# Routing attention and a PReLU feed-forward layer on one core: another order for seeded products, for the pairs' ordering, and for the weight conversions

## The chip, the cores and the metric

The kernel runs on one core of one Trainium2 chip. The metric is device time in microseconds (us) of one execution; the lower, the better. The engines are named as the profile names them: PE (TensorE matmuls), PEld (its weight loads), DVE (VectorE), ACT (ScalarE), POOL (GpSimd) and SP (SyncE, here a queue that issues DMAs). PE writes only to PSUM, which is dealt out in banks of 512 floats on 128 partitions. Each engine works through its own instructions in the order in which the program emits them; an instruction that waits holds all that stand behind it on the same engine.

## The reference

Attention in which a query sees only the keys of its own cluster, and then a feed-forward layer with a PReLU:

```python
B, H, S, D = 4, 8, 768, 64           # 16 clusters per head
q_assign = np.argmax(np.einsum('bhsd,hcd->bhsc', q_n, c_n), axis=-1)
k_assign = np.argmax(np.einsum('bhsd,hcd->bhsc', k_n, c_n), axis=-1)
mask = q_assign[:, :, :, None] == k_assign[:, :, None, :]
scores = np.where(mask, scale * np.matmul(q, k.transpose(0, 1, 3, 2)), -1e9)
attn = softmax(scores)
x = np.matmul(attn, v).transpose(0, 2, 1, 3).reshape(B * S, H * D)   # 3072 x 512
h = x @ w_in                                                          # 512 x 2048
out = (np.maximum(h, 0) + alpha * np.minimum(h, 0)) @ w_out           # 2048 x 512
```

q_n, k_n and c_n are q, k and the centroids, normalised. The weights and alpha come from the host in 64-bit floats (w_in, w_out as pairs of 32-bit words), and the kernel makes 32-bit floats of them on the chip.

## The kernel before

**Pairs and steps.** Work is cut into 16 pairs (a batch and two heads), four to a batch. The pairs n = 0 to 7 (batches 0 and 1, `NO = 8`) are done whole: each in two halves of the queries, each half in three steps. The pairs n = 8 to 15 (batches 2 and 3) are first brought into the order of their clusters; then a tile of queries only meets its neighbouring tiles of keys ("near"), and a pair takes three steps. So there are 72 steps, u = 0 to 71; pair n of the last eight starts at step 48 + 3(n - 8).

**Slots and ticks.** Everything is written out by hand in the order in which it is to be issued. `tick()` counts slots, runs what `later(slots, piece)` has put off, and issues up to two waiting loads. Steps 0 to 23 (the first part, batch 0) have five ticks each: scores (`score`, L815, masks L824, exponentials L833 and L836), then `weigh` of the step before (denominators L946, products with v L953), then three slots. When a half has ended, DVE turns its denominators (L959), inverts and spreads them (L965, L969, L926) and normalises (L1050); the next half's L946 needs the one denominator bank, and its L953 needs a bank back.

From step 24 on (`TOGETHER`) three steps make a group: the first begins with a head (three ticks: two thirds of the scores with the weighing of the pair before, its normalising, then the last third of the scores), followed by slots 3 and 4; the other two have slots 0 to 4. In every slot, after the due pieces, come one piece of the pair's own work, up to two pieces of `sorting`, in every third slot a weight conversion, and then pieces of the feed-forward layer of an earlier batch, as many as bring the rest down to the slot's share (`feed_down_to`). In a head step `prepare` runs before these pieces, in the other steps after them.

**Feed-forward.** The first product is done by Strassen's scheme in Winograd's form: for each pair of column blocks, seven products p1 to p7 of 768 columns (L1111) on three PSUM banks a, z, e. p1 fills a and ACT copies it to z (L1125); p6 adds onto a, p2 onto z, p5 fills e; p7 and p3 add onto a and e. DVE adds the results (L1096), ACT copies them out (L1130, L1134, L1139, L1157), and DVE applies the slope (L1100). p4 of a column pair, which adds onto a once DVE has read it, is kept pending and done within the next column pair, after three of its products (`settle`). The weights' sums come from DRAM, two forms to a load (`fetch_sums`, on ACT's queue), four such tiles in turn; a tile is fetched when an older one has been used up. The second product is L1183, in parts of four matmuls of 512 columns; `ps_f` has five banks for all of this, `ps_m` one (`misc`).

**Conversions.** `convert` loads raw words through SP's queue (L253) and makes floats in three pieces: split (DVE, L259 and L261), scale (ACT, L265 and L267), join (DVE, L271, L274, L277). In the first part one begins in each step: 16 blocks of w_in, whose sums `quarters` forms (L318) and stores, and then 8 blocks of w_out, 512 wide. In steps 24 to 47 follow 16 halves of 256 columns, one in every third slot, with two raw tiles.

**Ordering.** For the last eight pairs: `order_features` (L626), `order_sims` (L635, in the misc bank), `order_counts` (argmax L453 to L461, by cluster L644, running counts L649, one piece a slot), `order_begins` (L661, misc bank), `order_ranks` (L669 to L671), `order_rows` (L678 to L682) and `order_clusters` (L701 to L707), then `order_stage` (SP) and `order_scatter` (POOL, L728) through `sorting`; `order_load` fetches the rows back three steps before the pair starts, and `prep_clusters` (L493, misc bank) spreads the clusters. `ORDERS` holds the step at which each pair's ordering begins. In a head, `weigh_near`'s second side (L986) uses the misc bank until `normalise_near` (L992) has read it. `to_rows` (L1015, copied by L1018) and `put_back` (POOL, L1023) return a near pair's rows to their places.

**The end.** After step 71 the rest of batch 2's layer is dealt out while the last pair is put back; then batch 3's layer starts, some 25 small DVE instructions check that the assumptions held (L1441 to L1487), and one matmul (L1491) gathers the flag. If it fails, a general version runs; with these inputs it doesn't.

Of the kernel before, what the change touches and what calls it, by code (L numbers as in the profile page):

```python
# [23 lines left out]
def kernel(  # L24
# [68 lines left out]
    def later(slots, piece):  # L93
        due.setdefault(now[0] + slots, []).append(piece)
# [110 lines left out]
    for i in range(10):  # L205
        nc.tensor.matmul(out=warm[:, 0:P], lhsT=ident, rhs=ident, start=True, stop=True)

    inverses = const.tile([P, 2 * NCH, HS // Q], FP32, name="inverses")
    cn = inverses.rearrange("p n x -> p (n x)")[:, 0:D]
    cs2 = const.tile([P, 1], FP32, name="cs2")  # L210
# [123 lines left out]
    W_IN = len(sources) * 4  # L334
    for x0 in range(0, NQ, FQ):
        for f in (*range(x0, x0 + FQ), *range(NQ + x0, NQ + x0 + FQ)):
            n = CW if x0 == 0 else CW // 2
            for n0 in range(0, CW, n):
                sources.append((w_out_words[f * P:(f + 1) * P, 2 * n0:2 * (n0 + n)],
                                w_out_sb[:, f, n0:n0 + n], None))  # L340
# [6 lines left out]
        return coming.popleft()  # L347
    fetched, under_way = deque(), deque()
    begun, converted, first_ends = [0], [0], [1 << 20]
    limit = [W_IN + 2 * FQ]  # L350

    def fetch(ahead):

# [191 lines left out]
    def second_part():  # L545

        first_part.close()
        for name, bufs in (("gpool", NQ), ("ypool", NJ), ("emore", 1), ("ordc", 1),
                           ("ordp", 1), ("order", NCH + 2)):
            sorts[name] = fast.enter_context(tc.tile_pool(name=name, bufs=bufs))  # L550
        for i in range(2):
            e_tiles.insert(0, sorts["emore"].tile([P, 2, HS], FP32, name=f"more{i}"))
        fast.enter_context(middle)
        cvt[0] = middle.enter_context(tc.tile_pool(name="cvt2", bufs=2))
        raw2 = middle.enter_context(tc.tile_pool(name="raws2", bufs=1))
        raw_tiles[:] = [raw2.tile([P, CW // 2, 2], U32, name=f"raw{5 + i}") for i in range(2)]
        limit[0], first_ends[0] = W_IN + 2 * FQ + 4 * FQ, now[0]

    def third_part():
        middle.close()  # L560
# [79 lines left out]
    def order_counts(n, ps):  # L640

        top, first, pieces = argmax(ps, exact=True)
        member = sorts["ordp"].tile([P, HS], BF16, name="mine")
        pieces.append(lambda: nc.vector.transpose(  # L644
            out=member, in_=top.rearrange("p t c -> p (t c)")))

        def scan():
            count = sorts["ordp"].tile([P, HS], FP32, name="count")
            nc.vector.tensor_tensor_scan(count, member, member, 0.0, ALU.add, ALU.max)  # L649
            us[n] = member, count  # L650
        pieces.append(scan)
        for i, piece in enumerate(pieces):

            later(i if i < len(pieces) - 2 else i + 2, piece) if i else piece()
        later(len(pieces) + 4, lambda: order_begins(n))

    def order_begins(n):
        member, count = us[n]
# [38 lines left out]
    def order_clusters(n, begin):  # L697
        ordp, order = sorts["ordp"], sorts["order"]

        begun = ordp.tile([P, HS], BF16, name="mine")  # L700
        nc.vector.tensor_scalar(out=begun, in0=sorts["place"], scalar1=begin[:, 0:1],  # L701
                                scalar2=None, op0=ALU.is_ge)
        begunT = asg.tile([P, 2 * NX, NC], BF16, name="top")
        nc.vector.transpose(out=begunT.rearrange("p t c -> p (t c)"), in_=begun)
        first = order.tile([P, 2 * NX], BF16, name="cluster")
        with nc.allow_low_precision(reason="integers up to 16"):
            nc.vector.tensor_reduce(out=first, in_=begunT, axis=AX.X, op=ALU.add)  # L707
        firsts[n] = first
# [82 lines left out]
    waiting, weighed = [], {}  # L791
    e_tiles = [epool.tile([P, 2, HS], FP32, name=f"E{i}") for i in range(2 * GROUP)]

    def score(n, half, chunks):


        qkT = qkTs[n]
# [13 lines left out]
        for c, ps in zip(chunks, pss):  # L811
            tokens, m = queries(c)
            for h in range(2):
                r = h * D
                nc.tensor.matmul(  # L815
                    out=bank(ps, h, m),
                    lhsT=qkT[r:r + D, S + c * P:S + (c + 1) * P],
                    rhs=qkT[r:r + D, tokens], start=True, stop=not early_mask)
        if early_mask:
            for h in range(2):  # L820
                for c, ps in zip(chunks, pss):
                    g, i = divmod(NJ + c, GT)
                    r = slice(g * Q, (g + 1) * Q)
                    nc.tensor.matmul(  # L824
                        out=bank(ps, h), lhsT=members[n][1][r, h, i * P:(i + 1) * P],
                        rhs=aqs[n, half][r, 0, :], start=False, stop=True)
# [162 lines left out]
    def normalise_near(n):  # L989
        outT = inp.tile([P, 2, NJ, D], FP32, name="qk").rearrange("p h j d -> p (h j d)")  # L990
        for side in range(2):
            nc.vector.tensor_tensor(out=outT[:, side * HS:(side + 1) * HS],  # L992
                                    in0=pos.pop((n, side))[:, 0:HS],
                                    in1=rds.pop((n, side)), op=ALU.mult)
        whole = tc.dram_tile([2 * S, D], FP32, name=f"back{n}")
        to = dram_disjoint_views(whole, 2 * NJ)
        found = orders.pop(n)
        place = sorts["order"].tile([P, 2, NJ], I32, name="place")
        nc.vector.tensor_scalar(out=place, in0=found[:, :, :, 0], scalar1=0, scalar2=S - 1,
                                op0=ALU.max, op1=ALU.min)  # L1000
        rows = sorts["byrow"].tile([P, NJ, P], FP32, name="rows")

        starts = (6, 9)
        for i in range(2):
            later(starts[i], lambda i=i: to_rows(outT, rows, i))
            for x in range(NJ):
                later(starts[i] + 2 + x // 2,
                      lambda i=i, x=x: put_back(to, place, rows, i * NJ + x))
        later(starts[1] + 2 + HJ, lambda: fetch_back(n, whole))
# [69 lines left out]
    def ffn_pieces(b):  # L1079
# [23 lines left out]
        def hidden(x):  # L1103
# [14 lines left out]
            def p1():  # L1118
# [4 lines left out]
                    gs[f] = sorts["gpool"].tile([P, 2, HS], FP32, name="gT")  # L1123
                product(a, A11, B11, True)
                nc.scalar.copy(bank(z), bank(a))  # L1125
                rest.extend([p6, p2, p5, settle] if pending else [p5, p6, p2])

            def p6():
                product(a, S2, T2, False)
# [108 lines left out]
    FREE = SLOTS * SB - 3  # L1238


    ORDERS = [24, 27, 30, 33, 39, 42, 45, 48]
    prep_at, load_at = {}, {}
    for (n, half), u in start_of.items():
        def at(step, slot, piece):
            prep_at.setdefault((step, slot), []).append(piece)
        if half is None:
            t = ORDERS[n - NO]
            load_at.setdefault(t, []).append(lambda n=n: load(n))
            for i in range(2):
                at(t + 2, 2 + 2 * i, lambda n=n, i=i: order_features(n, i))  # L1250
            at(t + 3, FIRST + 1, lambda n=n: order_sims(n))
            load_at.setdefault(u - 3, []).append(lambda n=n: order_load(n))
            at(u - 4, 0, lambda n=n: prep_clusters(n))
            for i in range(2):
                at(u - 1, i, lambda n=n, i=i: order_blocks(n, i))
                at(u - 1, FIRST + i, lambda n=n, i=i: order_queries(n, i))
# [59 lines left out]
    for u in range(-AHEAD, TOGETHER):  # L1316
# [6 lines left out]
        if u >= 0:  # L1323


            score(n, half, (s, s + SB))
        tick()
        if ended:
            invert(*prior[:2])
# [4 lines left out]
        for i in range(SLOTS - FIRST):  # L1334
# [1 line left out]
            if (u, i) == (1 - AHEAD, 0):  # L1336
                cT, alpha = prepare_constants()
            prepare(u, FIRST + i)
            if u >= 0 and i == 0:
                convert_next()  # L1340
            if u >= -2:
                fetch(3)
# [123 lines left out]
    for i in (1, 3):  # L1466
# [19 lines left out]
                            axis=AX.X, op=ALU.max)  # L1486
    nc.vector.tensor_scalar(out=good[0:m, 1:2], in0=good[0:m, 0:1], scalar1=2.0 * P,  # L1487
                            scalar2=good[0:m, 1:2], op0=ALU.is_le, op1=ALU.mult)
    feed(2)
    flag = misc()  # L1490
    nc.tensor.matmul(out=flag[0:1, 0:1], lhsT=good[:, 1:2], rhs=ones[:, 0:1],  # L1491
                     start=True, stop=True)
# [168 lines left out]
```

## Time and profile before

| | us |
|---|---|
| median of three runs | 1011.37 (1011.29 to 1011.68) |
| the profiled execution | 1006.05 |
| its span, first to last instruction | 1004.3 |

Busy time over that span, from the windows of the trace (us):

| stretch | PE | DVE | ACT | POOL | granted clock of PE |
|---|---|---|---|---|---|
| 0 to 25 | 18.39 | 9.19 | 11.22 | 4.76 | 0.86 |
| 100 to 125 | 20.98 | 24.19 | 14.37 | 0.55 | 0.86 |
| 200 to 225 | 21.12 | 18.72 | 6.92 | 3.17 | 0.89 |
| 275 to 300 | 21.05 | 20.00 | 8.95 | 18.58 | 0.93 |
| 400 to 425 | 21.43 | 23.27 | 5.68 | 18.05 | 1.00 |
| 450 to 475 | 16.30 | 20.84 | 6.70 | 13.11 | 0.93 |
| 500 to 525 | 21.35 | 18.40 | 4.54 | 16.76 | 0.86 |
| 825 to 850 | 20.58 | 11.64 | 2.56 | 0.00 | 0.93 |
| 900 to 925 | 25.00 | 0.00 | 3.66 | 0.00 | 1.00 |

How to read it: a stretch in which PE is busy for less than its 25 us holds waits of PE; a clock of 0.86 means that PE ran at half its full speed for some 7 of the 25 us. Lines of the profile name the source line (L1111), the tile written and the tiles read, and in brackets the idle time before an instruction with what ended it. A matmul of 32-bit floats shows as two records.

### The profile page before, as it was taken

To read this page: it belongs to the slowest core of one execution; us is meant where nothing else is said; L and a number is where in the kernel's file an instruction comes from. 1 tells how busy PE (TensorE), PEld (TensorE's weight loads), DVE (VectorE), ACT (ScalarE), POOL (GpSimd) and SP (SyncE) were. 2 spreads that over 40 slices of the span, in tenths; PEclk is the share of its full clock that TensorE was granted. 3 is DMA by queue.
4 is the path that set the end of the run, shared out by engine and by line. 5 is a ranking of instruction groups with operands and counts; after the bars stand their busy time and mean duration, and the time that the engine had idled before them with its cause. 6 is when DMAs were issued, how large, how long until landed. Compare 5 with 4: busy or idle time off the path is not lost.

```text
span 1004.3 us, 11691 instructions
## 1 busy us (share of the span) xinstructions
PE 934.8 (93%) x3971; PEld 457.6 (46%) x3971; DVE 587.1 (58%) x1110; ACT 284.4 (28%) x566; POOL 320.9 (32%) x385
## 2 busy tenths in 40 slices
PE   7999899889989999896989899999999998999997
PEld 4444344434445444453445554455445444544544
DVE  3799998777884558968462966974513214300220
ACT  4767574324243311122212321222212001201200
POOL 1000001016675763645767577404022040000000
PEclk8999899999999999998989999999999999999999
DMA  5497955556546754765263735653004121301201
GB/s 201 132 293 216 252 126 137 125 103 136 130 126 143 169 126 109 159 154 132 69 126 91 175 89 114 120 128 100 15 19 118 52 71 56 96 9 32 73 22 45
DMA packets 276099, 115.26 MB, mean 115 GB/s; under 512 B 229296, under 2 KB 249024, under 8 KB 276032
## 3 DMA queue, kind: packets, MB, share of 16 engines
q1 hardware_dynamic: 247056, 63.12, 29.5%
q10 hardware_dynamic: 19760, 35.57, 12.1%
q0 software_dynamic: 9216, 15.75, 4.8%
q8 instruction: 33, 0.54, 0.2%
q14 instruction: 34, 0.28, 0.1%
HBM read 83.98 MB, written 30.41 MB: 114 GB/s over the span
## 4 chain that ended last, share of the span: by engine, by line
PE 72%; DVE 16%; DMA 4%; ACT 2%; issue 2%; POOL 2%; SPq 1%; ACTq 0%; DVEq 0%; POOLq 0%
PE fps L1183 29%; PE fps L1111 25%; PE fps L953 5%; PE sps L815 4%; PE fps L815 3%; DMA form<-sums 1%; PE fps L986 1%; PE sps L824 1%; DVE E L856 1%; POOL scratch L728 1%; PE mps L986 1%; DVE acc L866 1%; DVE xT L1088 1%; ACT fps L1125 1%; PE fps L946 1%
## 5 line engine op out<-in xcount | busy, mean ns | idle before, releaser
L1183 PE MATMUL fps<-w_out_sb,gT 128*128 128x512 f32 x752 | 333.6, 599 | 0.0
L1111 PE MATMUL fps<-xT,form 128*128 128x384 f32 x896 | 307.4, 498 | 25.5 <-ACT fps L1125 12.9
L728 POOL DMA_INDIRECT scratch<-stage,off x192 | 201.9, 1052 | 179.0 <-DMA stage<-in_v_dram 53.6
L1111 PEld LDWEIGHTS fps<-xT,form 128*128 128x128 f32 x896 | 168.0, 193 | 154.7 <-ACT fps L1125 25.8
L1183 PEld LDWEIGHTS fps<-w_out_sb,gT 128*128 128x128 f32 x752 | 141.5, 192 | 173.1 <-issue 168.6
L1023 POOL DMA_INDIRECT back<-rows,place x96 | 95.6, 996 | 165.3 <-ACT rows L1018 137.8
L1100 DVE SCALAR_TENSOR_TENSOR gT<-gT,alpha 128x768 f32<-128x768 f32 x64 | 63.7, 1010 | 96.1 <-ACT gT L1157 95.1
L1096 DVE TENSOR_TENSOR gT<-gT,fps 128x384 f32<-128x384 f32 x64 | 34.7, 548 | 96.8 <-PE fps L1111 96.8
L815 PE MATMUL sps<-qkT 64*128 64x384 f32 (+1 forms) x288 | 64.1, 523 | 2.8 <-ACT E L836 1.9
L953 PE MATMUL fps<-E,vt 128*64 128x384 f32 x320 | 61.8, 508 | 3.6 <-DVE xT L1050 3.6
L836 ACT ACTIVATE E<-sps 128x768 f32<-128x768 f32 (+1 forms) x56 | 43.9, 783 | 72.2 <-PE fps L824 55.5
L815 PE MATMUL fps<-qkT 64*128 64x384 f32 x288 | 59.9, 499 | 0.0
L1194 DVE TENSOR_TENSOR y<-y,fps 128x512 f32<-128x512 f32 x23 | 15.6, 677 | 67.0 <-PE fps L1183 67.0
L833 ACT ACTIVATE E<-fps 128x384 f32<-128x384 f32 x112 | 48.1, 493 | 11.7 <-PE fps L815 11.7
L1192 ACT COPY y<-fps 128x512 f32<-128x512 f32 x24 | 14.1, 586 | 122.2 <-PE fps L1183 122.2
L1125 ACT COPY fps<-fps 128x384 f32<-128x384 f32 x32 | 14.8, 463 | 109.3 <-PE fps L1111 73.6
L856 DVE SCALAR_TENSOR_TENSOR E<-aq,key,E 128x384 f32<-128x384 bf16 (+1 forms) x64 | 33.4, 578 | 13.5 <-ACT E L836 11.2
L815 PEld LDWEIGHTS sps<-qkT 64*128 64x128 f32 x288 | 23.3, 192 | 35.3 <-issue 12.2
L568 POOL IOTA place<- 128x384 uint16 x1 | 0.5, 458 | 113.1 <-DVE w_out_sb L274 113.1
L815 PEld LDWEIGHTS fps<-qkT 64*128 64x128 f32 x288 | 28.3, 192 | 16.8 <-issue 1.2
L1157 ACT COPY gT<-fps 128x384 f32<-128x384 f32 x32 | 15.3, 479 | 69.3 <-PE fps L1111 54.3
L953 PEld LDWEIGHTS fps<-E,vt 128*64 128x64 f32 x320 | 19.7, 138 | 31.4 <-issue 26.1
(184 smaller groups left out, 923.3 us busy)
## 6 DMA issues: line engine op xcount, KB each, us to landing
form<-sums ACTq DMA_DIRECT2D x112, 256.0 KB, 2.8
raw<-in_moe_w_in_dram SPq DMA_DIRECT2D x16, 512.0 KB, 6.5
sums<-forms SPq DMA_DIRECT2D x28, 256.0 KB, 4.7
qk<-scratch SPq DMA_DIRECT2D x64, 96.0 KB, 3.5
out_dram<-y ACTq DMA_DIRECT2D x23, 256.0 KB, 2.0
qk<-in_q_dram SPq DMA_DIRECT2D x48, 96.0 KB, 4.3
qk<-in_k_dram SPq DMA_DIRECT2D x48, 96.0 KB, 3.7
raw<-in_moe_w_out_dram SPq DMA_DIRECT2D x8, 512.0 KB
```

Source lines behind the costliest of these rows:

```text
L728: nc.gpsimd.indirect_dma_start(out=scratch[n][1][h * NX + xx], out_offset=bass.IndirectOffsetOnAxis(ap=ranks[n][:, xx, h:h + 1], axis=0), ...
L815: nc.tensor.matmul(out=bank(ps, h, m), lhsT=qkT[r:r + D, S + c * P:S + (c + 1) * P], rhs=qkT[r:r + D, tokens], start=True, stop=not early_ ...
L833: nc.scalar.activation(out=E[:, h, 0:m], in_=ps[h][:, 0:m], func=AF.Exp, scale=SCALE)
L836: nc.scalar.activation(out=E[:, :, 0:m], in_=ps[:, :, 0:m], func=AF.Exp, scale=SCALE)
L856: nc.vector.scalar_tensor_tensor(out=e, in0=of, scalar=keys[n][:, NJ + c, h:h + 1], in1=e, op0=ALU.is_equal, op1=ALU.mult)
L953: nc.tensor.matmul(out=po[r:r + D, 0:HS], lhsT=vts[n][:, h, c, :], rhs=e[:, h, :], start=(i == 0), stop=(i == NJ - 1))
L1023: nc.gpsimd.indirect_dma_start(out=to[i], out_offset=bass.IndirectOffsetOnAxis(ap=place[:, h, j:j + 1], axis=0), in_=rows[:, j, h * D:(h + ...
L1096: nc.vector.tensor_tensor(out=to, in0=to, in1=of, op=ALU.add)
L1100: nc.vector.scalar_tensor_tensor(out=g, in0=g, scalar=alpha[:, f:f + 1], in1=g, op0=ALU.mult, op1=ALU.max)
L1111: nc.tensor.matmul(out=bank(k), lhsT=w[:, cc, :], rhs=rhs[:, cc, :], start=start and cc == 0, stop=cc == KH - 1, skip_group_check=not start)
L1125: nc.scalar.copy(bank(z), bank(a))
L1183: nc.tensor.matmul(out=ps[:, 0:DM], lhsT=gs[f][:, half, t * P:(t + 1) * P], rhs=w_out_sb[:, f, :], start=on and f == fs[0], stop=off and f ...
```

## The change

- In a column pair with a pending p4 the order after p1 is p5, p6, p2, then the pending p4. Before, it was p6, p2, p5, and then p4.
- 26 matmuls (`warm_up`) are issued in step 0 between the scores and the masks, into the bank of the denominators.
- Of w_out, four blocks instead of eight are converted whole in the first part; in steps 0 and 1 two conversions begin instead of one. The other four blocks are converted in halves in steps 24 to 47, 24 halves in all instead of 16.
- `order_begins` comes four slots later after the counts; the tile by cluster is taken when it is written; `begunT` uses another buffer. The ordering of the last four pairs begins one step earlier, and where it then falls outside of a group's first step, the sims stand at slot 0. `prep_clusters` moves from slot 0 of the step four before the pair's start to the last slot of the step three before it. `to_rows` of the second half comes one slot sooner.
- Before the flag matmul, eight pieces of the layer are issued instead of two.

```diff
+    def warm_up():
+        for i in range(26):
+            nc.tensor.matmul(out=first_den[:, 0:P], lhsT=ident, rhs=ident, start=True, stop=True)
...
-            n = CW if x0 == 0 else CW // 2
+            n = CW if f < FQ else CW // 2
...
-    limit = [W_IN + 2 * FQ]
+    limit = [W_IN + FQ]
...
-        limit[0], first_ends[0] = W_IN + 2 * FQ + 4 * FQ, now[0]
+        limit[0], first_ends[0] = W_IN + FQ + 2 * (NF - FQ), now[0]
...
     def order_counts(n, ps):
         top, first, pieces = argmax(ps, exact=True)
-        member = sorts["ordp"].tile([P, HS], BF16, name="mine")
-        pieces.append(lambda: nc.vector.transpose(
-            out=member, in_=top.rearrange("p t c -> p (t c)")))
+        kept = []
+
+        def by_cluster():
+            kept.append(sorts["ordp"].tile([P, HS], BF16, name="mine"))
+            nc.vector.transpose(out=kept[0], in_=top.rearrange("p t c -> p (t c)"))
+        pieces.append(by_cluster)
 
         def scan():
+            member = kept[0]
...
-        later(len(pieces) + 4, lambda: order_begins(n))
+        later(len(pieces) + 8, lambda: order_begins(n))
...
-        begunT = asg.tile([P, 2 * NX, NC], BF16, name="top")
+        begunT = ordp.tile([P, HS], FP32, name="rd").bitcast(BF16)[:, 0:2 * NX * NC].rearrange(
+            "p (t c) -> p t c", c=NC)
...
-    def score(n, half, chunks):
+    def score(n, half, chunks, between=None):
...
+        if between is not None:
+            between()
         if early_mask:
...
-        starts = (6, 9)
+        starts = (6, 8)
...
-                rest.extend([p6, p2, p5, settle] if pending else [p5, p6, p2])
+                rest.extend([p5, p6, p2])
+                if pending:
+                    rest.append(settle)
...
-    ORDERS = [24, 27, 30, 33, 39, 42, 45, 48]
+    ORDERS = [24, 27, 30, 33, 38, 41, 44, 47]
...
-            at(t + 3, FIRST + 1, lambda n=n: order_sims(n))
+            at(t + 3, FIRST + 1 if t % SB == 0 else 0, lambda n=n: order_sims(n))
             load_at.setdefault(u - 3, []).append(lambda n=n: order_load(n))
-            at(u - 4, 0, lambda n=n: prep_clusters(n))
+            at(u - 3, FIRST + 1, lambda n=n: prep_clusters(n))
...
-            score(n, half, (s, s + SB))
+            score(n, half, (s, s + SB), warm_up if u == 0 else None)
...
-            if u >= 0 and i == 0:
+            if u >= 0 and i == 0 or u in (0, 1) and i == 2:
                 convert_next()
...
-    feed(2)
+    feed(8)
     flag = misc()
```

## The prediction

> **What bounds it now.** I read the busy shares first, then the clock row, then the list of what TensorE (PE) waited for, then the stretches where the long waits lie.
>
> ```profile
> PE 934.8 (93%) x3971; PEld 457.6 (46%) x3971; DVE 587.1 (58%) x1110; ACT 284.4 (28%) x566; POOL 320.9 (32%) x385
> ...
> PEclk8999899999999999998989999999999999999999
> ```
>
> PE is busy 934.8 of 1004.3 us. So 69.5 us of waits, and the half-clock stretches behind some of them (mean granted clock 0.976: 24 us at full speed lost if PE had work throughout), are all that an edit of order can win. Who was waited for:
>
> ```profile
> PE fps L1111 <- ACT fps L1125: 12.9, 20, 1.7
> PE fps L1111 <- DVE gT L1096: 12.6, 3, 5.9
> PE mps L661 <- DVE place L999: 7.3, 2, 3.7
> PE mps L635 <- DVE simT L453: 4.9, 2, 3.3
> PE mps L1491 <- DVE good L1487: 3.8, 1, 3.8
> PE fps L953 <- DVE xT L1050: 3.6, 3, 1.6
> PE sps L824 <- ACT outside L480: 3.3, 1, 3.3
> PE mps L493 <- ACT rows L1018: 3.2, 5, 0.9
> PE fps L946 <- DVE simT L959: 2.9, 2, 2.3
> PE mps L635 <- DVE begins L670: 1.9, 1, 1.9
> ```
>
> Columns: total us, times, longest. Nearly every row is something that the diff moves; I price them in turn.
>
> **The seeded bank, about -11.** p1 fills bank a, ACT copies it to bank z (L1125, 463 ns), and p6, which adds onto a, must not start before the copy is done. With a p4 pending, p6 is next:
>
> ```profile
> 858.12 9.30 PE L1111 MATMUL fps<-xT,form 128*128 128x384 f32 x28 [0.61 <-ACT fps L1125]
> ```
>
> 28 records in 9.30 us are seven products of 1.33 us. Now p5, on a fresh bank, stands between: 1.33 us of cover against 0.61. One wait of 1.65 (at 420.44) keeps some 0.3, and two at 156.77 and 188.30 are followed by waits for DVE at 165.85 and 202.31 which take up what is won (1.2). 12.9 - 0.3 - 1.2 = 11.4; I take 11. What is late next: p5 needs its form two products earlier. In the odd columns that form is fetched when p4 of the column before is done, three products (4.0 us) ahead; the form loads landed in 2.5 to 3.8 us, so it is just in time. Cover gone: 0.61 again, or up to 1 us each. Bounds -12.9 to 0.
> A rule against it: the Trainium skill, Perfetto Trace Analysis, Identifying Performance Opportunities, says that the same gap repeating on the engine that should be saturated can mean too few SBUF or PSUM tiles; then asking for the third bank two products sooner would lengthen the gap. By that rule this term is 0 or worse. The row names the copy as releaser and 0.61 is the copy plus a hand-over, so I go by the row.
>
> **Counts and broadcasts, about -11.** At the heads of steps 51 and 54 the matmul of order_begins (L661) wants the one misc bank, which still holds weigh_near's second side until DVE has masked and normalised; the last scores stand behind it.
>
> ```profile
> 450.34 1.95 PE L986 MATMUL mps<-E,vt 128*64 128x384 f32 x16
> ...
> 452.97 0.81 PE L815 MATMUL fps<-qkT 64*128 64x384 f32 x4
> 457.43 0.58 PE L661 MATMUL mps<-count,row 128*128 128x1 f32 x4 [3.65 <-DVE place L999]
> 457.94 1.45 PE L815 MATMUL fps<-qkT 64*128 64x384 f32 x4
> ...
> 475.72 2.93 PE L1111 MATMUL fps<-xT,form 128*128 128x384 f32 x4 [5.78 <-DVE gT L1096]
> ...
> 504.09 0.99 PE L661 MATMUL mps<-count,row 128*128 128x1 f32 x4 [3.65 <-DVE place L999]
> ...
> 507.44 2.93 PE L1183 MATMUL fps<-w_out_sb,gT 128*128 128x512 f32 x4
> ```
>
> ```profile
> 604.00:614.00 10.00, 8.26 (x22) 3.52 (x21) 4.90 (x8) 1.20 (x3) 7.70 (x9) 0.83 0.78 159
> 836.00:846.00 10.00, 6.18 (x16) 3.28 (x15) 4.51 (x26) 0.96 (x2) 0.00 (x0) 0.83 0.18 52
> ```
>
> (In these, the third figure from the end is the granted clock.) Four slots later, and with the sims of the second four pairs in the third step at slot 0, no order_begins lies in a head.
> Step 54: scores go on at 500.4 and the next L1183 starts at 501.8 instead of 507.44; 5.6, plus 1 us of half clock after it, less 0.6 for L661 itself elsewhere: -6.
> Steps 51-52: the products there end on DVE, which reaches L1096 at 475.12, 17.8 us after its last L999. Of that queue 3.7 (ranks, rows, clusters, L669 to L707) and 2.0 (L453 to L456) move a step earlier, 1.8 of idle goes, 1.5 (L644, L649) comes in, and L493 now waits at this head too. L1096 at some 469 to 470; less L635 and L661, which run elsewhere (1.5): -4.
> Step 48: the L670 wait goes, -1.9. Step 30: L453 stands behind 3.6 us of ranks and rows that now come later, -1.6. Step 36: the 3.34 splits: L635 waits 0.7, then L661 in step 37 waits behind the rest of prep_argmax (3.1), an add (0.95) and L453 (0.57), with only L635 (0.85) and p1 (1.33) before it, some 2.5: 0. Step 44: order_begins follows the sims by one slot that gets no product: +0.8.
> prep_clusters (L493): its old waits (3.2), and those of L1015 beside it (0.99 and 1.17) go. But its new place is the last slot of a head step, with the bank still held: L992 ends 5.0 us after L986's mps rows (452.3 to 457.3), while the scores end 2.6 us after them. In steps 57, 60 and 63 the sharing rule deals no product before it (step 54 and 66 get a part of 3.5 us): 3 x 2.4 = 7.3. Net +1.9.
> Sum: -6 - 4 - 1.9 - 1.6 + 0.8 + 1.9 = -10.8. Bounds: +4.5 (see the second rival) to -20 (every old wait and its half clock gone). The work itself is the same on every queue. Of the second four pairs the eight loads of 96 KB on SP's queue and the two L626 (0.96 each) come a step sooner, and the 18 stage loads and 24 scatters some three slots sooner; of the first four the latter come four slots later. They go two a slot, the fourth pair's end near step 46, and its load back is at 54, so nothing waits. The put-backs come one slot sooner on POOL, busy 32%; mine and begunT change buffers on DVE alone, in its own order: nothing.
> Clock: waits of 1.17 and 0.57 us at 606 to 607 were followed by 0.83 over 604 to 614, that is 1.7 us lost. By that row each of the three 2.4 us waits can cost 1.7; I count neither that (the second rival does) nor the 1.7 that may go. The Trainium skill (TensorE: Matmul & The Clock Gate, Why this matters for your kernels) asks only that PE not idle longer than about 3 us; by that rule these waits would cost no clock at all, and this trace differs.
>
> **Conversions, about 0.** First part: DVE is the bound there by turns. From L959 at 93.03 to L959 at 111.73 it works 18.70 us without idle while PE's L946 come 13.51 apart; the lateness of 5.2 showed as 2.29 + 1.62 = 3.91 of waiting, so 1.3 is slack, and the clock fell after it (mean 0.76 over 108 to 122: 3.4 lost). Conversions run at one a step as before, two steps ahead, and end at step 17. The four sums (2.61 us) leave that stretch and enter the one before step 12: 3.91 becomes about 1.4, the 0.31 at 81.94 about 2.4, and the 2.22 at 50 to 53 about 2.5 plus 0.3 earlier, as two more conversions of 2.6 lie ahead of it. 6.6 for 6.44 + 3.4: -3.3.
> Middle: eight more half conversions in steps 36 to 41, 1.8 us of DVE each, 14.6, where DVE is busy 46 of 75 us (275 to 350), and eight loads of 256 KB on SP's queue, ahead of the pair loads and the stage loads behind them. A load that is late holds DVE, and behind DVE the plus that p4 needs:
>
> ```profile
> 197.27 0.29 DVE L259 TENSOR_SCALAR power<-raw 128x256 uint32<-128x256 uint32 x1 [5.00 <-DMA raw<-in_moe_w_out_dram]
> ```
>
> That one gave PE's 5.87 at 202.31, which stays. DVE waited 7.7 us for 16 such loads; eight more: 3.9. I take +3 (0 to 30). The weights are joined before their first use: the last in the head of step 42, the first L1183 of that half in step 43.
>
> **Warm-up, 0.** 26 matmuls are 52 records (the ten at the outset show 20); at full clock eight took 1.21 us with the last one's tail, 0.115 each, so 6.0 us in a wait of 3.31. The masks start at 18.0 instead of 15.59, but the clock, 0.72 over 10 to 22 now, stays up: exp 0.81, scores 1.5 instead of 2.86, masks: step 1's L946 at 21.2, as before (21.19). Bounds -1 to +2.7.
>
> **The end, -5.5.** Eight products before the flag matmul instead of two cover its 3.81, and the 0.83 of 836 to 846 (1.7) goes. Bounds -5.5 to -3.
>
> **Sum.** -11 - 10.8 - 3.3 + 3 + 0 - 5.5 = -27.6 on a span of 1004.3. That execution took 1006.05, so 1.75 lies around the span, and the median of the runs is 5.3 above it; I carry both over: 1011.4 - 27.6 = 984.
>
> **Rivals.**
> 1. The seeded products find another wait (bank e not free, or the form late): term one is 0, 995. For it: 4.0 us against up to 3.8; against: five banks, four live. 0.08.
> 2. The freed bank waits come back: DVE sets steps 51 to 57, and each L493 wait also halves the clock (3 x 1.7). The order terms become -1.9 - 1.6 + 0.8 + 1.9 + 5.1 = +4.3: 999. For it: DVE is busy 23.3 of 25 us at 400 to 425; against: 4.9 of 25 at 525 to 550. 0.12.
> 3. More than I count: the 5.87 at 202.31 with its clock (7.5), and what is left at step 52 (4.7), go too: 971. 0.12.
> 4. Slower: raw loads in steps 36 to 41, each with the price of the one at 197.27 (5.87 + 1.65 = 7.5). From four on they eat the gain; five give 1021. For it: SP's queue is in order, with two raw tiles; against: after 206 only one of eight loads held DVE (2.67). 0.07.
> 5. All cancels, 1011: 0.03.
>
> **Numbers.** The forecast, 0.58, has its own range of 973 to 994. 968 to 1001 leaves out rival 4, no change, and the edges of rivals 2 and 3, some 0.2. About 0.2% (2 us) is what a measurement can tell from none. Faster 0.90 (forecast and rivals 1 to 3), same 0.03, slower 0.07.
>
> **What would show it.** Right: L1111 no longer waits for L1125, and p1, p5, p6 run on; L661 has no 3.65; L1491 has no wait; the clock row shows 9 in slices five, nineteen and twenty-one; L493 waits some 2.4 at three heads. Wrong: L1111 waiting for DVE or a form at p5; long idle before L259 between 275 and 340; L953 and L946 waiting more than 8 us in all before 140.

## The result, and the profile after

| | before | changed |
|---|---|---|
| median, six runs each (us) | 1011.19 (1009.74 to 1011.68) | 1023.33 (1019.13 to 1027.92) |
| ratio | | 1.012 (95% interval 1.0088 to 1.0153) |
| span of the profiled execution (us) | 1004.3 | 1019.7 |

The change makes the kernel slower by 1.2%; forecast was 984 us, a gain. Six of the runs below (a1, a2, a3, a5, e1, e2) met chips on which the kernel before itself took 1085 us, with waits of some 20 us that no kernel here shows elsewhere: only their ratios are given, and the weight lies on the others, where it took 1009 to 1010.

Lines have moved: L986 is now L997, L661 is L669, L635 is L639, L626 is L630, L493 is L497, L1015 and L1018 are L1026 and L1029, L815 is L824, L1096, L1111 and L1125 are L1107, L1122 and L1136, L728 is L737, L253 and L259 are L257 and L263, L717 is L726; L453 is L457, L919 is L930, L992 is L1003, L1073 (the loads of forms) is L1084, and the copies out L1130, L1134, L1139 and L1157 are L1143, L1147, L1152 and L1170. The page of the changed kernel, busy time and the granted clock in forty slices:

```profile
PE 943.8 (93%) x4023; PEld 467.7 (46%) x4023; DVE 589.4 (58%) x1130; ACT 285.1 (28%) x574; POOL 319.1 (31%) x385
...
PEclk9999999899989899999899989999999999999999
```

Of PE's 9.0 us more, 6.07 are the 52 records of the warm-up; the products L1122 and L1196 took 2.3 and 1.9 us more. What PE waited for (total us, times, longest):

```profile
PE fps L1122 <- DVE gT L1107: 21.9, 6, 8.4
PE mps L497 <- DVE qk L1003: 10.0, 4, 2.5
PE mps L639 <- DVE qk L630: 8.5, 4, 6.6
PE mps L1026 <- ACT rows L1029: 5.9, 2, 5.3
...
PE mps L669 <- DVE simT L457: 3.6, 3, 2.4
...
PE fps L1122 <- ACT fps L1136: 2.7, 1, 2.7
```

Of the rows shown of before, the copy's 12.9 us has become 2.7, the 7.3 of the begins behind a head is gone, and so is the flag's 3.8. In their place stand the clusters at the end of four heads (10.0), sims behind features (8.5), rows (5.9), and more waiting of products for DVE (12.6 has become 21.9). Where, in PE's order of time:

```profile
342.86 1.49 PE L639 MATMUL mps<-qk,cT 128*32 128x384 f32 x4 [6.57 <-DVE qk L630]
...
482.72 0.25 PE L497 MATMUL mps<-cluster,spread 128*128 128x24 bf16 x4 [2.48 <-DVE qk L1003]
...
599.82 2.93 PE L1122 MATMUL fps<-xT,form 128*128 128x384 f32 x4 [5.08 <-DVE gT L1107]
...
661.92 0.90 PE L1026 MATMUL mps<-ident,qk 128*128 128x128 f32 x3 [5.33 <-ACT rows L1029]
```

In the second the bank is held by the head's own products; in the other three a queue (DVE's, SP's, POOL's) is late, as the runs below show. The stretch of the old flag, by the windows (PE, PEld, DVE, ACT, POOL, then the granted clock), shows that part of the change at work: PE is busy throughout, at a granted clock of 1.00.

```profile
825.00:850.00 25.00, 25.00 (x64) 11.35 (x63) 3.01 (x5) 0.96 (x2) 11.52 (x12) 1.00 0.16 57
```

To see where time is lost, the same matmul of the scores was looked up in each profiled execution, and its start compared with that in the kernel before. In us, positive is late; the last column is the end of the span. (A step's place also moves with the products dealt before it, the same in all.) Each row is one execution; the medians of b2 and d3 lie 4.4 and 4.7 us above the executions profiled, so differences of a few us between rows carry little.

```
start before     142   211   278   315   345   402   453   500   553   592   626   649   717   end
changed         -0.6   0.9  -0.9   7.2  17.3  23.7  25.4  20.8  13.1  21.0  22.5  31.5  28.9  15.4
b2 (below)      -2.9  -2.9  -2.9  -1.6   1.7   1.7   0.9   2.6   3.2   2.6   5.0   5.0   2.4 -11.7
b3              +0.4   2.9   2.9   2.1   1.2   1.2   1.2   2.8   3.4   2.7   5.2   5.2   2.6  -9.3
c3               2.5   5.3   3.5   9.7   8.7   9.4   9.0   5.7  -0.7   6.8   9.9  18.5  15.9   4.0
c2              -2.9  -1.2  -1.2   5.4  11.7  15.1  15.0   9.0   1.4  11.2  11.4  11.5   9.0  -5.0
d1              -0.6   0.9  -0.9   0.2  10.4  16.8  14.3   8.4   0.7   0.0   0.8   5.1   2.6 -11.5
d2               0.2   1.3   1.3   2.2   5.3   5.3   2.4   4.2   4.9   4.1   1.0   1.0  -1.6 -14.0
```

The changed kernel loses 24 us between 278 and 402, wins 12 back in the heads between 453 and 553, where the prediction saw its gain, loses 18 between 553 and 649, and wins 13 after 717.

### The profile page after: what moved, and what is told of

Its sections match the earlier page's. It is cut to its first block, busy times and chain, and to the rows that moved or that the text cites. A ratio compares the mean times of both kernels' runs of the same rounds, so it can differ in the third digit from the quotient of the medians.

```text
span 1019.7 us, 11812 instructions
## 1 busy us (share of the span) xinstructions
PE 943.8 (93%) x4023; PEld 467.7 (46%) x4023; DVE 589.4 (58%) x1130; ACT 285.1 (28%) x574; POOL 319.1 (31%) x385
## 4 chain that ended last, share of the span: by engine, by line
PE 66%; DVE 17%; DMA 8%; SPq 3%; issue 2%; POOL 2%; ACT 1%; ACTq 0%; DVEq 0%; POOLq 0%
PE fps L1196 25%; PE fps L1122 22%; PE fps L964 4%; PE sps L824 3%; PE fps L824 2%; DMA scratch<-stage,off 2%; DVE gT L1111 1%; DVE acc L877 1%; DMA form<-sums 1%; SPq L133 1%; PE fps L997 1%; PE mps L997 1%; SPq L726 1%; DVE E L867 1%; DMA raw<-in_moe_w_out_dram 1%
## 5 line engine op out<-in xcount | busy, mean ns | idle before, releaser
L1196 PE MATMUL fps<-w_out_sb,gT 128*128 128x512 f32 x752 | 335.5, 602 | 0.0
L1122 PE MATMUL fps<-xT,form 128*128 128x384 f32 x896 | 309.7, 503 | 25.7 <-DVE gT L1107 21.9
L737 POOL DMA_INDIRECT scratch<-stage,off x192 | 199.5, 1039 | 217.7 <-DMA stage<-in_v_dram 91.0
L1122 PEld LDWEIGHTS fps<-xT,form 128*128 128x128 f32 x896 | 171.3, 195 | 150.3 <-DVE gT L1107 25.9
L1196 PEld LDWEIGHTS fps<-w_out_sb,gT 128*128 128x128 f32 x752 | 142.1, 193 | 170.4 <-issue 168.1
L1111 DVE SCALAR_TENSOR_TENSOR gT<-gT,alpha 128x768 f32<-128x768 f32 x64 | 63.6, 1012 | 65.9 <-ACT gT L1170 65.1
L1107 DVE TENSOR_TENSOR gT<-gT,fps 128x384 f32<-128x384 f32 x64 | 34.5, 547 | 87.0 <-PE fps L1122 87.0
L824 PE MATMUL sps<-qkT 64*128 64x384 f32 (+1 forms) x288 | 62.4, 510 | 4.8 <-ACT E L847 3.9
L824 PE MATMUL fps<-qkT 64*128 64x384 f32 x288 | 58.0, 488 | 0.0
L1136 ACT COPY fps<-fps 128x384 f32<-128x384 f32 x32 | 14.8, 463 | 98.6 <-PE fps L1122 76.6
L824 PEld LDWEIGHTS sps<-qkT 64*128 64x128 f32 x288 | 22.7, 188 | 40.3 <-ACT E L844 12.0
L847 ACT ACTIVATE more<-sps 128x768 f32<-128x768 f32 (+1 forms) x16 | 11.3, 704 | 104.7 <-PE sps L824 55.3
L867 DVE SCALAR_TENSOR_TENSOR E<-aq,key,E 128x384 f32<-128x384 bf16 (+1 forms) x64 | 33.2, 577 | 10.8 <-ACT E L847 10.8
L269 ACT ACTIVATE power<-power,low_exp 128x256 uint32<-128x256 uint32 (+1 forms) x44 | 26.8, 610 | 40.7 <-DVE power L263 40.4
L1170 ACT COPY gT<-fps 128x384 f32<-128x384 f32 x32 | 15.3, 479 | 75.7 <-PE fps L1122 59.2
L824 PEld LDWEIGHTS fps<-qkT 64*128 64x128 f32 x288 | 28.0, 189 | 17.4 <-ACT E L844 0.6
```

Source lines behind the costliest of these rows:

```text
L269: nc.scalar.activation(out=power[0], in_=power[0], func=AF.Relu, bias=low_exp[:, 0:1], scale=8.0)
L737: nc.gpsimd.indirect_dma_start(out=scratch[n][1][h * NX + xx], out_offset=bass.IndirectOffsetOnAxis(ap=ranks[n][:, xx, h:h + 1], axis=0), ...
L824: nc.tensor.matmul(out=bank(ps, h, m), lhsT=qkT[r:r + D, S + c * P:S + (c + 1) * P], rhs=qkT[r:r + D, tokens], start=True, stop=not early_ ...
L847: nc.scalar.activation(out=E[:, :, 0:m], in_=ps[:, :, 0:m], func=AF.Exp, scale=SCALE)
L867: nc.vector.scalar_tensor_tensor(out=e, in0=of, scalar=keys[n][:, NJ + c, h:h + 1], in1=e, op0=ALU.is_equal, op1=ALU.mult)
L1107: nc.vector.tensor_tensor(out=to, in0=to, in1=of, op=ALU.add)
```

## Experiments

**Which part costs: conversions or ordering (a1, a2, a3; b1, b2, b3).** From the changed kernel, the conversions (a1, b1), the ordering (a2, b2), or both (a3, b3) are put back as they were; the third run is thus the kernel before with seeded order, warm-up and the eight pieces alone.

```diff
 conversions (a1, b1; and a3, b3)
-            n = CW if f < FQ else CW // 2
+            n = CW if x0 == 0 else CW // 2
-    limit = [W_IN + FQ]
+    limit = [W_IN + 2 * FQ]
-        limit[0], first_ends[0] = W_IN + FQ + 2 * (NF - FQ), now[0]
+        limit[0], first_ends[0] = W_IN + 2 * FQ + 4 * FQ, now[0]
-            if u >= 0 and i == 0 or u in (0, 1) and i == 2:
+            if u >= 0 and i == 0:
 ordering (a2, b2; and a3, b3)
-        later(len(pieces) + 8, lambda: order_begins(n))
+        later(len(pieces) + 4, lambda: order_begins(n))
-    ORDERS = [24, 27, 30, 33, 38, 41, 44, 47]
+    ORDERS = [24, 27, 30, 33, 39, 42, 45, 48]
-            at(t + 3, FIRST + 1 if t % SB == 0 else 0, lambda n=n: order_sims(n))
+            at(t + 3, FIRST + 1, lambda n=n: order_sims(n))
-            at(u - 3, FIRST + 1, lambda n=n: prep_clusters(n))
+            at(u - 4, 0, lambda n=n: prep_clusters(n))
-        starts = (6, 8)
+        starts = (6, 9)
```

> The changed kernel, with the conversions of the kernel before: eight blocks of w_out whole in the first part, one conversion a step at the outset, 16 halves in the middle. Theory A (the eight additional raw loads hold SP's queue, so that stage loads, scatters and with them the pairs' loads come late): the waits for DVE at 282, 314, 600 and for the rows at 662 go, and their half clock; some 20 us, 995 to 1003. Theory B (the new places of the ordering's own pieces on PE's queue cost the time: L639 at slot 0 waits 6.6, four L497 wait 2.5 each, with their half clock): nearly all stays, 1015 to 1023.

> The changed kernel, with all of the ordering's pieces (counts, begins, sims, clusters, rows back) at the slots of the kernel before; seeded order, conversions, warm-up and the eight pieces before the flag stay changed. Theory A (conversions): the time stays above 1010, since the raw loads still hold SP's queue. Theory B (places of the ordering): some 995 to 1000, and no wait of L639 behind L630.

> The kernel before with only the seeded order, the warm-up and the eight pieces before the flag. Both theories: these three do what the prediction said: -11 and -5.5 and about 0, so 995 (990 to 1000), and no wait of a seeded product for the copy. If it is above 1005, the seeded order has a price that the trace of the changed kernel doesn't show as a wait of its own.

Measured on a chip of the long waits: a1 1.013 (0.996 to 1.031), a2 0.996 (0.989 to 1.002), a3 0.996 (0.989 to 1.003). Too wide to settle it, so the three were run again.

> The changed kernel with the conversions of the kernel before, again, since the first four runs met a chip on which every kernel, that of before too, took 6 to 8% longer with waits of up to 20 us behind late data. Theory A (additional raw loads in SP's queue): 995 to 1003. Theory B (places of the ordering's pieces): 1013 to 1022.

> The changed kernel with the ordering's slots of before, again. Theory A: over 1010. Theory B: 995 to 1002. In the disturbed runs it was 1.8% below the kernel with the conversions undone, which speaks for B.

> The kernel before with only the seeded order, the warm-up and the eight pieces before the flag, again: 995 (990 to 1000) by both theories.

Measured: b1 1015.27, ratio 1.0080 (1.0048 to 1.0113); b2 998.77, 0.9902 (0.9871 to 0.9932); b3 998.12, 0.9892 (0.9863 to 0.9921), the kernel before 1008.78 beside them. Theory A falls, and the ordering is what costs: 1.9% with the old conversions (b1 against b3) and 2.2% with the new ones (1.012 against b2). The conversions cost nothing that can be told with the old ordering (b2 against b3), and 0.4% with the new one (1.012 against b1), where the intervals overlap. The other three parts win 1.1%.

**Only the last four pairs' start and the sims' place (a5).** The lines of ORDERS and order_sims above are put back, alone.

> The changed kernel, with only the start of the last four pairs' ordering (39, 42, 45, 48) and with it the sims' place as before. Theory B: the wait of 6.6 us of L639 with its half clock, and the 1.3 and 0.5 beside it, go: 1008 to 1013. Theory A: the stage loads wait for the raw loads as much as now, and begin a step later: 1018 to 1028.

Measured: 1.0054 (1.0007 to 1.0101), on the same chip. Its profile has no wait of L639 for L630, as expected; the time stands between a1 and a2 there and decides nothing.

**The two named waits (b4).** Clusters back to their place, and the features of the last four pairs two slots sooner:

```diff
-                at(t + 2, 2 + 2 * i, lambda n=n, i=i: order_features(n, i))
+                at(t + 2, 2 * i + (2 if t % SB == 0 else 0), lambda n=n, i=i: order_features(n, i))
-            at(u - 3, FIRST + 1, lambda n=n: prep_clusters(n))
+            at(u - 4, 0, lambda n=n: prep_clusters(n))
```

> The changed kernel with the clusters spread where they were before (slot 0 of the step four ahead), and with the features of the last four pairs two slots earlier (slots 0 and 2), so that the sims at slot 0 of the next step stand further behind them. Theory B: L639's wait of 6.6 and its half clock go for the most part (2 slots of some 3 us), and the four of L497 (10 us) with 3.4 of half clock: 1000 to 1006. Theory A: these waits are made good by others, as SP's queue stays late: 1014 to 1022.

Measured: 1017.93, 1.0091 (1.0059 to 1.0124). Of the two rows' 18.5 us its list keeps 0.2 (the same two lines wait 2.4 for ACT in their place), and the time moved by 0.3%: theory B, as a sum of waits on PE's own order, falls. Products now wait for DVE 24.7 us instead of 21.9, rows 11.6 instead of 5.9, the copy 7.4 instead of 2.7. So something behind these engines seems to be late and to hand the same delay on.

**The four slots of order_begins (c1, c2, c3), and more pieces a slot (c4).** The ordering ends in `sorting`, a line of stage loads (SP) and scatters (POOL), first come, first served, two a slot. A pair adds 30 pieces, a group of three steps has 12 such slots (two in its head step, five in each other), so 24: with a pair in every group the line is never empty. Counted by the kernel's own rule, the first scatter of the eight pairs stands at these slots (all counted from the same step):

```
before, c1   180 198 216 234 255 273 291 309
changed, c3  184 202 223 241 259 277 298 316
c4           183 198 213 228 249 264 279 294
```

So with begins four slots later every scatter is 4 to 7 slots later, and that the last four pairs begin a step sooner doesn't change one of them.

```diff
 c1, c2
-        later(len(pieces) + 8, lambda: order_begins(n))
+        later(len(pieces) + 4, lambda: order_begins(n))
 c2 besides: the two edits of b4
 c3: b3 with one line of the change
-        later(len(pieces) + 4, lambda: order_begins(n))
+        later(len(pieces) + 8, lambda: order_begins(n))
 c4: the changed kernel with
-            for _ in range(min(2, len(sorting))):
+            for _ in range(min(3, len(sorting))):
```

> The changed kernel with order_begins four slots after the counts, as before, instead of eight; all else changed. The pieces of `sorting` go two a slot, 24 a group, a pair brings 30: the queue is full from the first pair on, so every scatter then stands at the slot of the kernel before, 4 to 7 slots sooner than now. Theory C (scatters 4 to 7 slots later are what costs, through POOL's and SP's queues, at the pairs' loads and the rows): ratio to before 0.990 to 0.997, the waits near 593 and 650 gone. Theory D (the places on PE's queue: L639 at slot 0, L497 at the end of a head): 1.006 to 1.012.

> The same, with the features two slots earlier for the last four pairs, and the clusters spread where they were before. Theory C: two waits of PE (6.6 and four of 2.5) go besides, 0.980 to 0.988. Theory D: these two are the price, and the four slots are nothing: as the run with these two alone, 1.005 to 1.010.

> Seeded order, warm-up and the eight pieces before the flag (0.989 of before), with order_begins eight slots after the counts as the one part of the ordering that is changed; the scatters then stand at the slots of the changed kernel. Theory C: 1.002 to 1.010. Theory D: 0.983 to 0.991, as L669 no longer waits 3.65 twice.

> The changed kernel with up to three pieces of `sorting` in a slot instead of two; scatters then stand 3 to 26 slots sooner, ahead of those of the kernel before from the second pair on. Theory C: below 1.000, with the loads back and the rows in time. Theory D: 1.008 to 1.015. A third outcome: POOL and SP take the pieces no faster than now, and their queues only hold them longer: 1.008 or more with longer waits on SP.

Measured, with the kernel before at 1009.0: c1 1013.03, 1.0034 (1.0013 to 1.0055); c2 1001.53, 0.9935 (0.9918 to 0.9951); c3 1008.27, 0.9987 (0.9968 to 1.0005); c4 1045.66, 1.0377 (1.0353 to 1.0402). The four slots cost 0.9% in the changed kernel (1.012 to c1) and 1.0% alone (b3 to c3), although c3 has no wait of L669 for a head any more. Features and clusters, worth 0.3% while the scatters stood late, are worth 1.0% with them in place (c1 to c2). So c1, c2 and c3 all end between what theories C and D expected: each theory has a part of the price. And "late scatters" as such falls with c4: there they stand up to 22 slots sooner than in the changed kernel, the last of them ran at 598 us instead of 642, and it is the slowest of all. Its longest wait, first in PE's and then in ACT's order of time:

```profile
605.87 0.90 PE L1026 MATMUL mps<-ident,qk 128*128 128x128 f32 x3 [12.67 <-ACT rows L1029]
```

```profile
605.34 0.48 ACT L1029 COPY rows<-mps 128x384 f32<-128x384 f32 x1 [14.20 <-DMA back<-rows,place]
```

A pair's rows are written back by POOL between the scatters; with more scatters ahead of them the tile isn't free, and ACT and then PE stand. This is one part of c4's loss only: at the scores of 453 us, before any row goes back, it is already 36.8 us late, and the waits before that (4.14 for ACT at 281.62, 7.81 for DVE at 321.16) were not followed to their source. What decides seems to be how this traffic is mixed with the rest of the two queues, and not only how early it is.

How a stage load reaches PE can be followed in c3. ACT in order of time, then SP:

```profile
306.13 0.49 ACT L1143 COPY gT<-fps 128x384 f32<-128x384 f32 x1
312.15 0.33 ACTq L1084 DMA_DIRECT2D form<-sums  x1
312.52 0.48 ACT L1147 COPY gT<-fps 128x384 f32<-128x384 f32 x1 [5.90 <-DMA stage<-in_q_dram]
```

```profile
309.82 0.60 SPq L726 DMA_DIRECT2D stage<-in_q_dram  x1
310.46 0.62 SPq L726 DMA_DIRECT2D stage<-in_k_dram  x1
```

The records of the instructions name the semaphores (start us, us):

```
309.692  0.028  Sync    EVENT_SEMAPHORE  L726   $S[114]>= $S[113]>=
309.757  0.027  Sync    EVENT_SEMAPHORE  L726   $S[102]>= $S[112]>=
309.817  0.596  Sync    DMA_DIRECT2D     L726   stage<-in_q_dram   $S[111]>= semaphore=102
312.072  0.038  Scalar  EVENT_SEMAPHORE  L1084  $S[102]>= $S[100]>=
312.148  0.326  Scalar  DMA_DIRECT2D     L1084  form<-sums         $S[108]>= semaphore=102
```

Semaphores 111 to 118 are those of POOL's scatters and rows back. SP's load waits for scatters to free the stage tile; ACT's load of a form, which needs no stage, takes the next turn on semaphore 102 and so waits until SP's load has landed; behind it in ACT's queue stand the copies that free the products' banks, and PE waits 4.65 us for DVE at 315.05.

**Without the stage loads (d1, d2).** In both, the 144 loads of q, k and v into the stage tiles are left out and the tiles are zeroed once; d1 is else the changed kernel, d2 the same with the ordering of b2.

```diff
+        for t in stage:
+            nc.gpsimd.memset(t, 0.0)
...
-        for src, p0, d0 in ((q, 0, 0), (k, TS, 0), (v, TS, D)):
-            nc.sync.dma_start(out=t[p0:p0 + TS, :, d0:d0 + D],
-                              in_=src[b, head, rows].rearrange("(x p) d -> p x d", p=TS))
```

> The changed kernel without the 144 loads of q, k and v into the stage tiles (the scatters move zeros and the row numbers, so the last eight pairs attend over zeros). Theory E (the stage loads in SP's queue carry the ordering's price): it ends 0 to 10 us above the next run. Theory D (PE's and DVE's own order): 18 to 27 us above it, as with the loads.

> The same without the stage loads, with the ordering's slots of before. Both theories: a little below the run with the loads, 0.980 to 0.990; it is the measure for the run above.

Measured: d1 994.90, 0.9860 (0.9837 to 0.9884); d2 990.56, 0.9808 (0.9779 to 0.9836). The price of the changed ordering falls from 2.2% to 0.5%: some 17 of its 22 us come through the stage loads, be it their place in the queues or the data that they move. The waits of PE's own order are all still there in d1 (lines moved by one or two; L497, then the sims, in its list of waits):

```profile
PE mps L497 <- DVE qk L1002: 10.0, 4, 2.5
PE mps L641 <- DVE qk L632: 8.5, 4, 6.5
```

They have a price, too: between 315 and 402 d1 loses 16.6 us, d2 3.1. But the heads win 13.6 against it (table, 453 to 553), and 0.5% is left. What is gone or halved are the losses at 315, 592 and 649.

The loss at 592 in the changed kernel shows the way through SP itself. SP, then DVE, in order of time:

```profile
588.08 0.60 SPq L726 DMA_DIRECT2D stage<-in_q_dram  x1
588.72 0.61 SPq L726 DMA_DIRECT2D stage<-in_k_dram  x1
589.38 0.61 SPq L726 DMA_DIRECT2D stage<-in_v_dram  x1
590.18 3.04 SPq L133 DMA_DIRECT2D qk<-scratch  x2
```

```profile
595.63 0.98 DVE L764 STREAM_TRANSPOSE qkT<-qk 128x768 f32<-128x768 f32 x1 [9.66 <-DMA qk<-scratch]
```

The last of the pair's loads back stand behind six stage loads (583.36 to 590.00), on a queue that had stood 13.4 us for scatters, until 570.21, and was working off what lay behind. In its list of waits between 540 and 571:

```profile
SPq L726 <- DMA scratch<-stage,off: 21.0, 3, 13.4
```

Between 583 and 594 SP waits no more for a tile, but 5.1 us in all for its turns behind other loads, 4.3 of them behind ACT's forms. DVE stands 9.66 us for the load back, and the add that frees a bank (L1107) stands behind DVE's transpose: 5.08 us of PE.

**Better mixtures (d3, d4).** Both are built on b3: two conversions in steps 0 and 1, but all eight blocks of w_out in the first part; d4 has begins two slots after the counts besides.

```diff
 d3, d4
-            if u >= 0 and i == 0:
+            if u >= 0 and i == 0 or u in (0, 1) and i == 2:
 d4
-        later(len(pieces) + 4, lambda: order_begins(n))
+        later(len(pieces) + 2, lambda: order_begins(n))
```

> The kernel before with the seeded order, the warm-up, the eight pieces before the flag, and two conversions a step in steps 0 and 1, while all eight blocks of w_out stay in the first part, and the ordering as before. The traces show the two at the outset win 3.3 us by 124 us, and the middle's eight halves cost 3.8 by 340; without the latter 0.989 becomes 0.986 (0.983 to 0.988). Rival: the sums' DVE work only moves, 0.988 to 0.992.

> The same, with order_begins two slots after the counts instead of four: at steps 51 and 54 L669 then stands ahead of the head's use of the bank instead of behind it, so two waits of 3.65 with 6.8 of half clock go, and every scatter comes two slots sooner. If the scatters' slots stand well in SP's and POOL's queues: 0.972 to 0.980. Rival: the ranks' and rows' DVE work then delays the masks of the head, or SP's queue gives it back as it did for the four slots later: 0.985 or more.

Measured: d3 996.20, 0.9875 (0.9851 to 0.9899); d4 1005.72, 0.9972 (0.9947 to 0.9997). d3 has the best time of the kernels that compute the whole, faster than before and than the change; from b3 and b2 it can't be told apart. d4 gives 1.0% away against d3: L669 no longer waits for the head (7.4 us in d3), but six times for DVE's reading of the denominators from the same bank:

```profile
PE mps L669 <- DVE inverses L930: 12.7, 6, 4.7
```

So four slots is not a point on a slope; two (d4 against d3) and eight (c3 against b3) are both worse.

**The stage loads from POOL's queue (e1, e2).** The changed kernel, and d3, with one word changed:

```diff
-            nc.sync.dma_start(out=t[p0:p0 + TS, :, d0:d0 + D],
+            nc.gpsimd.dma_start(out=t[p0:p0 + TS, :, d0:d0 + D],
```

> The changed kernel with the stage loads issued by POOL instead of SP. If their place in SP's queue is what costs: SP's raw and pair loads and ACT's form loads go on, 0.986 to 1.000. If it is the data or POOL's own time: 144 more issues on POOL, ahead of its scatters and the rows back, 1.010 or more, with the waits for rows (L1026 for L1029) longer.

> The version with two conversions at the outset and the ordering as before (0.9875), with the stage loads issued by POOL. Queue: 0.980 to 0.987. POOL's own time: 0.990 or more.

Measured on a chip of the long waits: e1 0.9694 (0.9614 to 0.9774), e2 0.9630 (0.9567 to 0.9692). The two are 0.7% apart, with intervals that overlap, where the changed kernel and d3 are 2.5% apart with the loads on SP. It points to the place in the queue and not to the data moved; but neither kernel ran on a chip where the one before takes 1010 us, so this is not shown, and their size stays open.

## Why the prediction failed, by its own steps

- **Seeded bank, -11: the mechanism right, the size off.** The row of 12.9 us is 0.6 in b3. It pays where PE is the bound: after 717 b3 wins 11.9 us (2.6 to -9.3); taking 5.5 of it as the flag's, some 6.4 are left. Nine waits of 0.61 stood there (5.5 us), of which two of 0.79 and 0.65 remain; the rest is in no wait's row. Before 717 the banks are freed sooner and the same steps end no sooner: the wait at 202.31, which the prediction left at 5.87, starts sooner and lasts 8.11 in b3, with 10.2 us of half clock, and the rows at 611.56 wait 3.84. The rule weighed against this term, a repeated gap for want of banks, didn't come to bear: p5 waited but twice, 0.79 for a form (778.03) and 0.65 behind ACT's copy (939.24).
- **Warm-up, 0: right.** b3 is 0.3 late at 30 us; the clock over the first 25 us is 1.00 instead of 0.86, and no time is won by it.
- **The end, -5.5: right as far as it shows**: the flag's wait is in no list after the change, and the row 825 to 850 has PE busy at a clock of 1.00. No run has this part alone.
- **Conversions, 0: right in the sum, with some luck in the terms.** b2 against b3 wins 3.3 at 142 (-2.9 against +0.4), as forecast, but 5.8 by 211; between 278 and 345 it loses 6.3 (from -5.8 to +0.5) where +3 was taken and 0 to 30 allowed. Both terms are about twice as large, and they cancel: the medians are 0.65 us apart.
- **Counts and broadcasts, -10.8 with bounds of +4.5 and -20: this failed, with some +22.** Two of its terms were right: the heads of steps 51 and 54 give 12.3 us (25.4 to 13.1; -6 and -4 were forecast), and the clusters wait 2.48 at the heads' ends, four times where three were forecast. Two steps were not. First, "the work itself is the same on every queue": the sims at slot 0 stand right behind the features of the step before, and these, on DVE, behind the ranks and rows that order_begins had moved there. DVE in order of time:

```profile
337.57 0.18 DVE L690 TENSOR_SCALAR off<-rank 128x24 int32<-128x24 f32 x1
...
338.62 0.55 DVE L716 TENSOR_REDUCE cluster<-rd 128x24 bf16<-128x384 bf16 x1
...
341.83 0.97 DVE L630 STREAM_TRANSPOSE qk<-qk 128x768 f32<-128x768 f32 x1
```

  PE waited 6.57 us for this second L630, and 0.19, 0.52 and 1.25 for others. The ranks are not all of it: with begins at their old place (c1) the four waits still come to 6.4. That was not priced at all, and it costs some 13.5 us by 402 even without stage loads (d1 against d2), which the heads then give back. Second, and larger, "the 18 stage loads and 24 scatters some three slots sooner ... so nothing waits". The line takes 24 pieces a group where a pair brings 30; nothing comes sooner, all come 4 to 7 slots later, and the loads beside them on SP's queue and on its shared turns (raw words, pairs, forms, rows) are late in turn. Without the stage loads, 17 of the 22 us are gone. The four slots by themselves are some 9 of them (c1, c3); the others seem to need the new places of the second four pairs' pieces besides: POOL's scatters wait 91.0 us for stage loads in the changed kernel, 78.7 in c1, but 55.9 in c3 and 53.6 before.
- **The rivals.** The fourth had the sign, and one of its marks is there, 7.61 us of DVE idle before L263 at 280.17; but b1, with eight raw loads fewer, is still 0.8% slower than before. Its place, SP's queue, was right; the loads that decide there are those of the stages, which the prediction had put at nothing.
- **What stays open:** the remaining 0.3% between c2 and b2, whose intervals overlap (the rows one slot sooner, the last pairs' loads a step sooner), was not divided further, nor was c2's loss of 16.3 us between 278 and 402, most of which it wins back by 553. What an early place in the line costs (c4), and whether the stage loads cost by their place or by their data, is not shown.

## What to carry to other kernels

A piece that is moved by some slots moves everything it feeds: count the line it joins (what it takes a round, what comes in), and price its DMAs against every load that shares their queue or their turns. When a named wait is taken away and the time stays, look for the late queue behind it. An edit made of many moves is best split before it is judged: here three parts win 1.1%, a fourth nothing, and the fifth loses twice as much.

## What the runs showed of the hardware

- All DMAs that SP and ACT issue in the changed kernel use the same eight semaphores, 100 to 107 (SP 54 to 61 each, ACT 14 to 21 each), in turns; 521 of these 599 show a wait for the very semaphore that they use next, that is, for the landing of the last DMA on it. So an engine's queue can stand 5.90 us for a load of another engine that it has nothing to do with (c3, 306 to 312).
- In the changed kernel the granted clock falls to 0.50 during or right after long waits of PE, for 3.41 us or a multiple: 10.24 with the wait of 8.45 that ended at 201.92, 6.83 with those of 6.57 and 5.08, 3.41 with that of 5.33 (661.92), and 3.41 with two of the four waits of 2.48 to 2.54 (from 569.76 and from 617.55). The Trainium skill (TensorE: Matmul & The Clock Gate, Why this matters for your kernels) asks that PE not idle longer than about 3 us. These two waits were shorter, and the clock fell all the same, which at half speed costs up to 1.7 us each; after the other two it did not.
